# A list schedule in the source for the second mixture and the rest of the last layer 2

## The chip, the cores and the metric

The kernel runs on one core of a Trainium2 chip. The metric is the device time of one execution in microseconds (us). Five engines work side by side, each through its own instruction list in order: PE (TensorE, matmuls), DVE (VectorE), ACT (ScalarE), POOL (GpSimd, which here mostly issues indirect transfers) and SP (which issues the plain transfers). An instruction waits on semaphores that other engines or transfers raise; everything behind it on the same engine waits with it.

## The reference

```python
x = attention(q, k, v)            # B4 H8 S576 D64, causal, window 64, -> (2304, 512)
x = moe(x)                        # 8 experts, weights by Sinkhorn, every expert on every token
# second mixture: each token goes to one expert, at most cap tokens for each
N, D, E, F = (2304, 512, 8, 1024)
cap = N // E                      # 288
logits = x @ w_gate
order = np.argsort(-logits.flatten())
for idx in order:
    tok, e = (int(idx) // E, int(idx) % E)
    if assigned[tok] >= 0 or counts[e] >= cap:
        continue
    assigned[tok] = e
    counts[e] += 1
for e in range(E):
    mask = assigned == e
    h = np.maximum(x[mask] @ w1[e], 0.0)
    out[mask] = h @ w2[e]
```

## The kernel before

Tokens lie in 18 row tiles of 128. Attention and the first mixture take the first 1598 us; they work in blocks of 384 tokens, three products in float16 halves for each product of the reference. The change concerns the rest, called the tail here:

- **The gate of the second mixture.** When the first mixture's last expert has finished a row tile, `gate2` transposes it (L986 on PE, the copy L987 on ACT), multiplies it with the gate's weights (L991) and copies the logits (L992 on DVE); `to_rows` normalises it (L998 on ACT, a chain of small DVE operations L312 to L317, L1005 and L1006 on ACT, L1008 on POOL) and stores it as rows of two float16 halves, `xrows`. For the last six tiles `held_logits` computes the logits ahead from the hidden values (L1052 and L1054 on PE, L1056 to L1059 on DVE), so that routing can begin while 126 matmuls of the last layer 2 (L943) still stand on PE.
- **`route(ph)`** assigns 288 tokens to one expert, the one that fills first, in each of eight phases. Masked logits (L1114 to L1136), then six rounds of a search for a threshold: a comparison `G` of 128x720 on DVE (L1146, L1148), 18 small matmuls on PE that count (L1152), two small DVE operations (L1154, L1155), small matmuls that broadcast the new bound (L1159). Then counts (L1171), the expert's number `widx` (L1185), a prefix sum (L1217), slots (L1221 to L1231), one-hot rows (`oh` L1233, `rh` L1237), 18 matmuls that turn them into row numbers (L1241), `idx` (L1253), three gathers of 96 rows each on POOL (L1258), 24 transposes on PE in three groups of 8 (L1277), and three copies into `xgt`, one on DVE (L1279) and two on ACT (L1281).
- **`ffn(ph)`** has 96 matmuls of layer 1 (L1302) and 96 of layer 2 (L1314), each of 128x288. **`put(ph)`** transposes the result back in three groups (L1324), scales it on ACT (L1326) and stores it with an indirect transfer on POOL (L1328).
- **The weights of an expert** come by four indirect gathers of 1 MB on POOL (L1193) into one of two sets of buffers: the two of layer 1 as soon as `widx` is known, the two of layer 2 behind the three row gathers.

What sets the order: up to the line `man.close()` the source's own list schedule (tasks, each with requests for an engine, a cost and the events on which it waits) emits the instructions. Behind it the framework's scheduler orders what the source emits, and `man.close()` stands ahead of `held_logits` and `second`, so that the tail is in the scheduler's order. It is there that L943 stands between the held logits, and that the rounds of route `ph+1` stand between the matmuls of `ffn(ph)`.

## Time and profile before

| | before |
|---|---|
| median of 3 runs | 1947.3 us (1940.54 to 1947.51) |
| profiled execution, its own time | 1943.79 us |
| its span, first to last instruction | 1942.0 us |
| mean granted clock of TensorE | 0.988 |
| PE busy | 1859.8 us, 96% |
| DVE busy | 1261.4 us, 65% |
| ACT busy | 916.1 us, 47% |
| POOL busy | 110.8 us, 6% |

The shares are means over the whole span; the tail from 1598 us on is 18% of it and has limits of its own. A busy PE includes the time in which the last matmul ahead of a wait runs out of the pipeline. The profiled execution lies 3.5 us under the median of the runs.

### The profile page before, as it was taken

How to read it: one execution, taken by the hardware profiler on the slowest of the kernel's cores; microseconds unless marked ns; L12 is line 12 of the kernel's file. 1: busy time of each engine (PE TensorE's matmuls, PEld its weight loads, DVE VectorE, ACT ScalarE, POOL GpSimd, SP SyncE). 2: the span in 40 equal slices, each digit the busy share in tenths (PEclk: the TensorE clock that was granted, in tenths of full speed). 3: DMA queues.
4: the chain of work that ended last, by engine and by line, in shares of the span. 5: the costliest groups of instructions: out<-in, count | busy, mean ns of one | idle time of the engine just before them, and what ended most of it. 6: DMA issues, size and time to landing. Idle time of an engine off the chain costs nothing.

```text
span 1942.0 us, 39658 instructions
## 1 busy us (share of the span) xinstructions
PE 1859.8 (96%) x15605; PEld 1339.3 (69%) x15605; DVE 1261.4 (65%) x3845; ACT 916.1 (47%) x2493; POOL 110.8 (6%) x142
## 2 busy tenths in 40 slices
PE   6899999999999999999999999999999997899987
PEld 5777755776686766767766867677686773676765
DVE  7877796464666676676667666766747777465540
ACT  6777634552455555554554555455534442222222
POOL 0000000000000000000000000000000113223231
PEclk9999999999999999999999999999999998899999
DMA  8465301140134323323442434234231101435451
GB/s 188 89 131 120 83 1 44 59 160 1 55 120 143 119 93 118 138 88 116 145 136 83 131 117 145 93 99 157 88 104 28 43 20 64 175 123 172 159 211 29
DMA packets 172795, 203.32 MB, mean 105 GB/s; under 512 B 83000, under 2 KB 130104, under 8 KB 168512
## 3 DMA queue, kind: packets, MB, share of 16 engines
q1 hardware_dynamic: 164928, 157.78, 27.4%
q0 software_dynamic: 7680, 43.02, 6.3%
q8 instruction: 122, 2.00, 0.4%
q14 instruction: 65, 0.53, 0.1%
HBM read 143.05 MB, written 57.71 MB: 103 GB/s over the span
## 4 chain that ended last, share of the span: by engine, by line
PE 71%; DVE 11%; issue 6%; DMA 5%; ACT 4%; POOL 2%; SPq 0%; POOLq 0%; ACTq 0%; DVEq 0%
PE p L943 28%; PE p L865 17%; PE pb L865 12%; PE p L1302 4%; PE p L773 3%; DMA w2scr<-st2k 2%; DVE st2k L347 1%; DMA raw<-xrows,idx 1%; PE pb L1152 1%; DVE xl L645 1%; PE p L1314 1%; DMA raw<-in_moe_w_dram 1%; DMA ws<-st2k 1%; PE pb L632 1%; DVE pn L605 1%
## 5 line engine op out<-in xcount | busy, mean ns | idle before, releaser
L943 PE MATMUL p<-w2b,hh 128*128 128x512 f16 x2304 | 686.0, 379 | 0.0
L943 PE MATMUL p<-w2b,hl 128*128 128x512 f16 x1152 | 436.6, 379 | 0.0
L943 PEld LDWEIGHTS <-hh 128*128 128x128 f16 x2304 | 222.1, 99 | 218.2 <-issue 0.2
L865 PEld LDWEIGHTS <-w1b 128*128 128x128 f16 x4032 | 340.3, 98 | 22.2 <-issue 4.0
L865 PEld LDWEIGHTS <-w1x 128*128 128x128 f16 x3024 | 256.3, 98 | 21.1 <-issue 7.4
L865 PE MATMUL p<-th,w1x 128*128 128x192 f16 x1344 | 221.2, 246 | 4.3 <-ACT sa L877 2.2
L865 PE MATMUL pb<-xh,w1b 128*128 128x192 f16 x1344 | 221.3, 246 | 0.0
L943 PEld LDWEIGHTS <-hl 128*128 128x128 f16 x1152 | 112.6, 98 | 135.5 <-issue 0.6
L865 PE MATMUL pb<-xl,w1b 128*128 128x192 f16 x672 | 165.3, 246 | 0.0
L865 PE MATMUL p<-tl,w1x 128*128 128x192 f16 x672 | 165.3, 246 | 0.0
L347 DVE SCALAR_TENSOR_TENSOR st2k<-raw,wsc,st2k 128x512 f16<-128x512 f32 x128 | 91.9, 748 | 51.8 <-ACT st2k L345 51.5
L345 ACT ACTIVATE st2k<-raw,wsc 128x512 f16<-128x512 f32 x128 | 86.5, 713 | 71.3 <-DMA ws<-st2k 58.8
L959 DVE SCALAR_TENSOR_TENSOR acc<-p,SE,acc 128x512 f32<-128x512 f32 x126 | 94.0, 746 | 38.2 <-PE p L943 37.8
L1008 POOL TENSOR_TENSOR st2k<-tmp,st2k 128x512 f16<-128x512 f32 x18 | 24.7, 1370 | 1592.2 <-ACT tmp L1006 1571.1
L746 ACT ACTIVATE hh<-sb 128x192 f16<-128x192 f32 x168 | 61.0, 363 | 111.8 <-DVE sb L909 111.8
L865 PE MATMUL p<-th,w1b 128*128 128x192 f16 x672 | 110.6, 246 | 2.9 <-ACT sc L898 2.9
L746 ACT ACTIVATE hh<-sa 128x192 f16<-128x192 f32 x168 | 60.9, 363 | 107.2 <-DVE sa L883 107.2
L865 PE MATMUL pb<-xh,w1x 128*128 128x192 f16 x672 | 110.6, 246 | 0.0
L865 PE MATMUL p<-xh,w1b 128*128 128x192 f16 x672 | 110.6, 246 | 0.0
L883 DVE TENSOR_TENSOR sa<-pb,sa 128x192 f32<-128x192 f32 x168 | 60.0, 357 | 75.1 <-PE pb L865 72.6
L747 DVE SCALAR_TENSOR_TENSOR hl<-sa,hh 128x192 f16<-128x192 f32 x168 | 60.3, 359 | 72.1 <-ACT hh L746 72.1
L747 DVE SCALAR_TENSOR_TENSOR hl<-sb,hh 128x192 f16<-128x192 f32 x168 | 60.3, 359 | 71.7 <-ACT hh L746 71.7
(309 smaller groups left out, 3381.3 us busy)
## 6 DMA issues: line engine op xcount, KB each, us to landing
raw<-in_moe_w_dram SPq DMA_DIRECT2D x128, 512.0 KB, 5.6
ws<-st2k SPq DMA_DIRECT2D x128, 256.0 KB, 4.5
w2b<-w2scr SPq DMA_DIRECT2D x28, 512.0 KB, 7.1
w2scr<-st2k SPq DMA_DIRECT2D x48, 256.0 KB, 4.5
xrows<-st2k SPq DMA_DIRECT2D x18, 257.0 KB, 3.3
vs<-in_v_dram SPq DMA_DIRECT2D x35, 128.0 KB, 4.1
ldq<-in_q_dram SPq DMA_DIRECT2D x16, 256.0 KB, 4.6
ldk<-in_k_dram SPq DMA_DIRECT2D x16, 256.0 KB, 4.8
```

What stands on the lines that cost most here:

```text
L345: A.activation(hi, src, AF.Copy, scale=sc)
L347: V.scalar_tensor_tensor(lo, src, sc, hi, op0=OP.mult, op1=OP.subtract)
L605: V.tensor_tensor_reduce(pn[:, b, hp], pss[:, hp], mk, 1.0, -3.0e38, OP.add, OP.max, mx[:, u:u + 1])
L746: A.activation(hh[:, f, cols], src, AF.Relu)
L747: V.scalar_tensor_tensor(hl[:, f, cols], src, 0.0, hh[:, f, cols], op0=OP.max, op1=OP.subtract)
L773: PE.matmul(p[:, 0:w], w1v[wi][:, c, fs], x[:, c, ts], start=(n == 0), stop=(n == 3 * DC - 1))
L865: PE.matmul(bank[:, 0:HB], aq[wi][:, c, fs], xq[xi][:, c], start=(start and n == 0), stop=(n == 5), skip_group_check=True)
L883: V.tensor_tensor(t, b3[:, 0:HB], t, OP.add)
L943: PE.matmul(p, h[:, f, js], w2v[wi][:, f], start=(n == 0), stop=(n == 3 * FC - 1))
L959: V.scalar_tensor_tensor(acc[:, i], p, SE[:, e, i:i + 1], acc[:, i], op0=OP.mult, op1=OP.add)
L1008: G.tensor_tensor(xr[:, DM:2 * DM], xs, xr[:, 0:DM], OP.subtract)
L1302: PE.matmul(p[:, 0:CAP], wv1[f // 4][w][:, c, fs], xt[:, x * DC + c], start=(n == 0), stop=(n == 3 * DC - 1))
```

## The change

`man.close()` moves behind `second()`, so that the tail is emitted by the source's own list schedule, in the order of the source, with a cost for each step. For this `route` is cut into `route_a` (up to the slots), `weights_of` (all four gathers of an expert's weights, asked for as soon as `widx` is known) and `route_b` (one-hot rows to `xgt`); `ffn` asks for PE in units of three matmuls, `put` in three steps; the rest of the last layer 2 is a task of its own (`rest`). `to_rows` loses the second ACT copy and the POOL subtraction; one DVE operation of 128x512 does both. Some small operations of `route` move: `ob`, `cap` and `un` are updated ahead of the one-hot rows, `wi`, `wv` and `wp` ahead of the slots, `sv` behind the copies to `xgt`. The spacer's memset on POOL stands ahead of every store.

```diff
     def to_rows(i, x=1, dep=None):
...
+        a = yield Rq("ACT", 0.8, [dep])
         xs = rc["tmp"][:, x]
...
         A.activation(xr[:, 0:DM], acc[:, i], AF.Copy, scale=s)
-        A.activation(xs, acc[:, i], AF.Copy, scale=s)
-        yield 1
-        G.tensor_tensor(xr[:, DM:2 * DM], xs, xr[:, 0:DM], OP.subtract)
+        d = yield Rq("DVE", 0.75, [a.end], wait=0)
+        V.scalar_tensor_tensor(xr[:, DM:2 * DM], acc[:, i], s, xr[:, 0:DM], op0=OP.mult, op1=OP.subtract)
         SP.dma_start(xrows[i * 128:(i + 1) * 128, :], xr)
...
-        gather(*((0, x) for x in range(1 if ph == 0 else 2)))
         V.tensor_scalar(eo, eo, e8, None, op0=OP.is_equal)
-        yield 1
+        ft.add(weights_of(ph, widx, d.end), 2)
...
+    def weights_of(ph, widx, dep):
+
+        ws = wset2[ph % 2]
+        for m, a in ((0, 0), (0, 1), (1, 0), (1, 1)):
+            d = yield Rq("POOL", 1.2, [dep, ("free", ph - 2, m, a) if ph > 1 else "rest" if ph and m else None])
+            G.indirect_dma_start(out=ws[m][:, a * 4096:(a + 1) * 4096], out_offset=None, in_=wscr[m][a],
+                                 in_offset=bass.IndirectOffsetOnAxis(ap=widx[:, :1], axis=0))
...
         for j in range(NJ):
             x = xgb[(ph * NJ + j) % len(xgb)]
-            xd = G.indirect_dma_start(out=x, out_offset=None, in_=xrows[:, :],
-                                      in_offset=bass.IndirectOffsetOnAxis(ap=idx[:, j:j + 1], axis=0))
+            h = yield Rq("POOL", 1.2, [d.end] + [("xr", i) for i in HELD] + [("xgt", ph - 2)] * (ph > 1))
+            G.indirect_dma_start(out=x, out_offset=None, in_=xrows[:, :],
+                                 in_offset=bass.IndirectOffsetOnAxis(ap=idx[:, j:j + 1], axis=0))
...
-        rc["lastx"] = xd.ins
-        gather(*([(0, 1)] if ph == 0 else []), (1, 0), (1, 1))
...
+        ft.add(put(ph), 4)
...
+        ft.add(all_a(), RA)
+        ft.add(all_ffn(), 10)
+        ft.run(lambda: not ft.tasks)
...
     consts_route()
-    man.close()
     for b in range(NB - 2, NB):
         held_logits(b)
     bg.until("finish")
...
     second()
+    man.close()
     late.close()
```

How the instructions stand now is shown at three places.

**The start of the tail, on DVE.** `hs`, `hu` and `lg` take the held logits out of PSUM; `sw` and `tri` are constants of the routing, and `tri` is made from `jpr`, which POOL writes. Before:

```order
L1058 SCALAR_TENSOR_TENSOR hu<-pb,hs,lgh 128x8 x2
L1059 SCALAR_TENSOR_TENSOR lg_91<-pb,hs,hu 128x8
L747 SCALAR_TENSOR_TENSOR hl_82<-sb,hh_81 128x192
L1077 MEMSET sw 40x128 x3
L1059 SCALAR_TENSOR_TENSOR lg_91<-pb,hs,hu 128x8
L1056 TENSOR_SCALAR hs<-SE,gi 128x1 x2
L1058 SCALAR_TENSOR_TENSOR hu<-pb,hs,lgh 128x8 x2
L1059 SCALAR_TENSOR_TENSOR lg_91<-pb,hs,hu 128x8 x2
L1090 TENSOR_SCALAR tri<-jpr 128x128
```

After the change:

```order
L749 SCALAR_TENSOR_TENSOR hl_82<-sb,hh_81 128x192
L1082 MEMSET sw 40x128 x3
L1095 TENSOR_SCALAR tri<-jpr 128x128
L1097 MEMSET ones_19778 128x128
...
L1103 MEMSET AA 128x288
L1103 MEMSET zero 128x18
L1061 TENSOR_SCALAR hs<-SE,gi 128x1
L1063 SCALAR_TENSOR_TENSOR hu<-pb,hs,lgh 128x8
L1064 SCALAR_TENSOR_TENSOR lg_91<-pb,hs,hu 128x8
```

All six groups of `hs`, `hu` and `lg` now stand behind the constants; before, four of the six stood ahead of `tri`. Behind the six groups come three tiles of `gate2` and `to_rows` one after the other, where before one was left at this place, and then the first operation of routing (`lm`). This is the last of the three and the beginning of `lm`:

```order
L994 COPY lg_91<-pb 128x8
L314 TENSOR_SCALAR pbn<-x2m 128x1
L315 TENSOR_SCALAR pbn<-pbn 128x1
L317 TENSOR_SCALAR pcn<-pbn 128x1
L318 TENSOR_SCALAR x2s<-pcn 128x1
L319 TENSOR_SCALAR x2inv<-pcn 128x1
L1007 MEMSET st2k 128x2
L1008 COPY st2k<-x2inv 128x1
L1012 SCALAR_TENSOR_TENSOR st2k<-acc,x2s,st2k 128x512
L1126 TENSOR_TENSOR lm<-lg_91,ob 128x144
```

On PE the six tiles of held logits follow each other without an L943 (now L945) between them, then three times the transposes and the gate's matmuls of `gate2` (now L988, L993), then 30 matmuls of L945, and then the first 18 matmuls of a round.

**The end of a phase, on PE.** The rows are those of one of the middle phases; `pb<-rh,oh` are the 18 matmuls for the row numbers, `pb<-id,raw` a group of eight transposes of gathered rows, `pb<-A,G` a round's matmuls, `ident,yT` a group of `put`; of every run of equal rows the first stands here. Before, 48 matmuls of layer 2 lie between the row numbers' matmuls and the first transposes, three between the groups, and 15 behind the last; the round of the next phase follows:

```order
L1241 MATMUL pb<-rh,oh 96x6
...
L1314 MATMUL p_21612<-hh_81,w2b 128x288
...
L1277 MATMUL pb<-id_19879,raw 128x96
...
L1152 MATMUL pb<-A_21698,G 40x8
...
L1159 MATMUL pb<-fl,sw 128x1
```

After the change 24 matmuls of layer 2 follow the row numbers' matmuls, and the transposes stand in the next phase's first two rounds and `put`:

```order
L1171 MATMUL pb<-A_21612,G 40x8
...
L1413 MATMUL p_21682<-ident,yT 96x128 x4
L1180 LDWEIGHTS sw
L1180 MATMUL pb<-fl,sw 128x1
L1413 MATMUL p_21697<-ident,yT 96x128 x4
L1326 LDWEIGHTS raw
L1326 MATMUL pb<-id_19780,raw 128x96
...
L1413 MATMUL p_21746<-ident,yT 96x128 x4
...
L1383 MATMUL p_21790<-xgt_20013,xh 128x288
```

Behind the first two rounds' matmuls come the transposes of the first and the second group of rows, behind the last group of `put` those of the third, then the third round and layer 1. On DVE the copy of the second group (now L1330) stands between the second and the third `G`.

**The gathers of a phase, on POOL.** `xh`, `xl` (set 0) and `w1b`, `w2b` (set 1) are the weights' buffers, `raw` the gathered rows, `out_dram` the stores. Before:

```order
L1193 DMA w1b<-ws_121,widx 128x4096
L1258 DMA raw<-xrows,idx 96x1028 x3
L1193 DMA w2b<-ws_122,widx 128x4096
L1193 DMA w2b<-ws_123,widx 128x4096
L1328 DMA out_dram<-tmp,idx 2304x512 x3
L1193 DMA xh<-ws_120,widx 128x4096
```

After the change:

```order
L1284 DMA w1b<-ws_120,widx 128x4096
L1284 DMA w1b<-ws_121,widx 128x4096
L1284 DMA w2b<-ws_122,widx 128x4096
L1284 DMA w2b<-ws_123,widx 128x4096
L1316 DMA raw<-xrows,idx 96x1028 x3
L1421 MEMSET spacer 1x1
L1422 DMA out_dram<-tmp,idx 2304x512
```

The two gathers for layer 2 have moved from behind the row gathers to ahead of them, into one burst of four.

## Rows read from the trace of the kernel before

**Rows 1.** Windows: length, busy time of PE, PEld, DVE, ACT, POOL; clock, DMA share, GB/s.

```profile
1640.00:1650.00 10.00, 3.95 (x79) 3.18 (x79) 5.82 (x20) 1.33 (x2) 3.32 (x3) 0.54 0.09 30
1650.00:1660.00 10.00, 5.14 (x68) 3.93 (x68) 3.20 (x10) 1.62 (x2) 4.24 (x5) 0.50 0.82 294
...
1735.00:1770.00 35.00, 33.38 (x371) 24.85 (x370) 21.02 (x83) 8.57 (x17) 9.88 (x10) 1.00 0.45 155
```

**Rows 2.** PE's timeline at the head: start, length, operation, idle time before it.

```profile
1598.29 0.34 PE L1052 MATMUL pb<-w2h,hh 128*128 128x16 f16 x8
...
1609.67 0.61 PE L1152 MATMUL pb<-A,G 128*40 128x8 f16 x18 [0.38 <-DVE st2k L1004]
...
1626.48 0.22 PE L1171 MATMUL pb<-AG,ones 128*128 128x144 f16 x1
...
1637.81 0.97 PE L1241 MATMUL pb<-rh,oh 128*96 128x6 f16 x18 [1.23 <-DVE rh L1237]
...
1658.99 1.14 PE L1302 MATMUL p<-xgt,xh 128*128 128x288 f16 x4
```

**Rows 3.** The last `gate2` and its `to_rows`: timelines of ACT, PE and DVE.

```profile
1593.39 0.60 ACT L987 ACTIVATE tmp<-pb 128x512 f32<-128x512 f32 x1 [0.75 <-PE pb L986]
...
1595.13 0.95 PE L991 MATMUL pb<-wg2s,tmp 128*128 128x8 f32 x8
...
1596.12 0.17 DVE L992 COPY lg<-pb 128x8 f32<-128x8 f32 x1 [2.68 <-PE pb L991]
...
1596.95 0.72 ACT L1005 ACTIVATE st2k<-acc,x2s 128x512 f16<-128x512 f32 x1 [2.35 <-DVE x2s L316]
1597.58 0.70 ACT L1006 ACTIVATE tmp<-acc,x2s 128x512 f32<-128x512 f32 x1
```

**Rows 4.** DVE's timeline at the head, and POOL's first operation there.

```profile
1603.43 0.23 DVE L1090 TENSOR_SCALAR tri<-jpr 128x128 f16<-128x128 f32 x1 [1.93 <-POOL jpr L1089]
...
1605.06 0.74 DVE L959 SCALAR_TENSOR_TENSOR acc<-p,SE,acc 128x512 f32<-128x512 f32 x1
1605.72 0.30 DVE L1114 TENSOR_TENSOR lm<-lg,ob 128x144 f32<-128x144 f32 x1
...
1601.06 1.15 POOL L1008 TENSOR_TENSOR st2k<-tmp,st2k 128x512 f16<-128x512 f32 x1 [7.09 <-issue]
```

**Rows 5.** PE's timeline of one middle phase: its two heads and its waits.

```profile
1692.35 0.61 PE L1152 MATMUL pb<-A,G 128*40 128x8 f16 x18
...
1712.57 0.29 PE L1314 MATMUL p<-hh,w2b 128*128 128x288 f16 x1
1713.08 0.16 PE L1217 MATMUL pb<-tot,tri 128*128 128x2 f16 x1 [0.23 <-DVE tot L1214]
...
1717.63 0.97 PE L1241 MATMUL pb<-rh,oh 128*96 128x6 f16 x18 [0.30 <-DVE rh L1237]
...
1722.79 0.51 PE L1277 MATMUL pb<-id,raw 96*128 96x96 f16 x8 [0.49 <-DMA raw<-xrows,idx]
...
1723.92 0.52 PE L1277 MATMUL pb<-id,raw 96*128 96x96 f16 x8 [0.26 <-DMA raw<-xrows,idx]
...
1725.22 0.51 PE L1277 MATMUL pb<-id,raw 96*128 96x96 f16 x8 [0.42 <-DMA raw<-xrows,idx]
...
1727.51 0.61 PE L1152 MATMUL pb<-A,G 128*40 128x8 f16 x18
```

**Rows 6.** That phase's late copies to `xgt` (DVE, ACT), and POOL's gathers for layer 2.

```profile
1726.63 0.56 DVE L1279 COPY xgt<-pb 128x768 f16<-128x768 f16 x1 [2.57 <-PE p L1314]
...
1726.75 0.81 ACT L1281 ACTIVATE xgt<-pb 128x768 f16<-128x768 f16 x1 [2.60 <-PE p L1314]
...
1723.25 0.96 POOL L1193 DMA_INDIRECT xl<-ws,widx  x1 [0.31 <-issue]
```

**Rows 7.** PE's two long waits of the last phases, from its timeline.

```profile
1870.76 1.63 PE L1302 MATMUL p<-xgt,xh 128*128 128x288 f16 x12 [2.36 <-ACT xgt L1281]
1886.16 0.50 PE L1277 MATMUL pb<-id,raw 96*128 96x96 f16 x8 [3.27 <-ACT xgt L1281]
```

More of the change, by code (lines that the diff above doesn't have):

```diff
@@ L961, in layer2 @@
                 finals.append(i)
-            if i == NT - 1 and not out:
+            if i == NT - 1 and not out and "out" not in rc:
                 bg.done.add(("l2x", e))
@@ L998, in to_rows @@
         A.activation(xs, acc[:, i], AF.Square, accum_out=m)
+        d = yield Rq("DVE", 1.0, [a.end], wait=1.5)
         s = small.tile([128, 1], F32, name="x2s")
@@ L1277, in route, with ws_of, evac_h, evac_y @@
                 PE.transpose(pt[:, c], xg[j][:, c * 128:(c + 1) * 128], rc["id16"][0:R, 0:R])
+            fr = ("l1", ph - 2) if ph > 1 else None
             if j % 2:
+                d = yield dv(0.82, p.end, fr)
                 V.tensor_copy(xt[:, :, j * R:(j + 1) * R], pt)
             else:
+                d = yield Rq("ACT", 0.81, [p.end, fr])
                 A.activation(xt[:, :, j * R:(j + 1) * R], pt, AF.Copy)
-            yield 1
-        PH[ph] = (xt, ws, idx, sv)
+            ft.release("psx", p.idx, d.end)
+        ft.at["xgt", ph] = d.end
+        yield dv(0.5)
+        for j in range(NJ):
+            V.tensor_tensor(sv[:, j:j + 1], xg[j][:, 2 * DM:2 * DM + 2].bitcast(F32), wp[0:R], OP.mult)
+        PH[ph] = (xt, ws_of(ph), idx, sv)
+        ft.at["rows", ph] = d.end
+    def ws_of(ph):
+        return wset2[ph % 2]
     xgb, xgt, otb, yTb, wset2 = [], [], [], [], []
     stores = []
-    def ffn(ph, before):
+    def evac_h(ph, f, p, e):
+        hh, hl = [t[:, :, 0:CAP] for t in hbuf[ph % 2]]
+        a = yield Rq("ACT", 0.42, [e.end])
+        A.activation(hh[:, f], p[:, 0:CAP], AF.Relu)
+        d = yield dv(0.46, a.end)
+        V.scalar_tensor_tensor(hl[:, f], p[:, 0:CAP], 0.0, hh[:, f], op0=OP.max, op1=OP.subtract)
+        ft.release("ps1", e.idx, d.end)
+        ft.at["hb", ph, f] = d.end
+    def evac_y(ph, d, p, e, idx):
+        a = yield Rq("ACT", 0.42, [e.end, ("put", ph - 1) if ph else None])
+        A.activation(yTb[0][:, d], p[:, 0:CAP], AF.Copy)
+        ft.release("ps2", idx, a.end)
+        ft.at["y", ph, d] = a.end
+    def ffn(ph):
+        while ("rows", ph) not in ft.at:
+            yield IDLE
         xt, ws, idx, sv = PH[ph]
@@ L1324, in put @@
                 PE.transpose(p[0:R, d * 128:(d + 1) * 128], yT[:, d, j * R:(j + 1) * R], ident)
+            if j == NJ - 1:
+                ft.at["put", ph] = e.end
+            a = yield Rq("ACT", 0.68, [e.end], "ot")
             ot = otb[(ph * NJ + j) % len(otb)]
             A.activation(ot, p[0:R], AF.Copy, scale=sv[:, j:j + 1])
+            ft.release("ps2", e.idx, a.end)
+            g = yield Rq("POOL", 1.3, [a.end])
             G.memset(rc["spacer"], 0.0)
@@ L1332, in put, with evac_rest, rest @@
             stores.append(st)
-            yield
+    def evac_rest(i, p, t, idx):
+        d = yield dv(0.75, t)
+        V.scalar_tensor_tensor(acc[:, i], p, SE[:, E - 1, i:i + 1], acc[:, i], op0=OP.mult, op1=OP.add)
+        ft.release("ps2", idx, d.end)
+        x = len(finals) % 2
+        e = yield from to_rows(i, i % 2, d.end)
+        ft.at["xr", i] = e + 3.6
+    def rest():
+        k = 12 - pend[0][1]
+        tick = rc["tick"]
+        for g, n in ((pend[0][0], k), (layer2(E - 1, NB - 1), 12)):
+            for x in range(12 - n, 12):
+                e = yield Rq("PE", 1.31, [], "ps2" if x % 4 == 0 else None)
+                if x % 4 == 0:
+                    tick[0] = e.idx
+                rc["pe"] = e
+                next(g)
+        for _ in g:
+            pass
     def second():
@@ L1351, in second, with all_a, all_ffn @@
             rc[n] = late.enter_context(tc.tile_pool(name=n, bufs=x, space=PSUM))
-        first = route(0)
-        for x in first:
-            if x == "rows":
-                break
-        rest()
-        def route_all():
-            for ph in range(E):
-                for _ in first if ph == 0 else route(ph):
-                    yield 1
-                bg.done.add(("r", ph))
-                yield 1
-        bg.start("route", route_all())
-        before = iter(())
-        for ph in range(E):
-            bg.until(("r", min(ph + 1, E - 1)))
-            ffn(ph, before)
-            before = put(ph)
-        for _ in before:
-            pass
+        assert not bg.tasks, bg.tasks
+        bg.hold = True
+        rc["tick"] = [0]
+        ft.rel["ps2"].append(None)
+        rc["out"] = lambda i, p: ft.add(evac_rest(i, p, rc["pe"].end, rc["tick"][0]), 1)
+        def all_a():
+            for ph in range(E):
+                while ("begun", ph - AHEAD) not in ft.at and ph >= AHEAD:
+                    yield IDLE
+                yield from route_a(ph)
+        def all_ffn():
+            yield from rest()
+            ft.at["rest"] = rc["pe"].end
+            for ph in range(E):
+                ft.at["begun", ph] = ft.t
+                yield from ffn(ph)
+        ft.at["free", -1, 0, 0] = 0.0
+        ft.add(all_a(), RA)
+        ft.add(all_ffn(), 10)
+        ft.run(lambda: not ft.tasks)
+        del rc["out"]
     wgr = abase.tile([128, DC, E], F32, name="wgr")
```

183 lines of the change are left out of this document (114 added, 69 removed).

## The prediction

> **What bounds the kernel now.** I read the windows first, to find where PE is not full, then PE's timeline in those stretches, and then the engine that each of its waits names. Up to 1598 us nothing of weight changes: PE is full there, and the edits move work on ACT, POOL and DVE beside it. The tail has three parts. In the head PE stands half idle: of the twenty microseconds from 1640 to 1660 it is busy for 9.1, at a granted clock of 0.54 and 0.50, the lower level (1.2 GHz of 2.4) [rows 1]. The routing of phase 0 is a chain there: first round at 1609.67, counts at 1626.48, row numbers at 1637.81, layer 1 at 1658.99 [rows 2]. Then come five middle phases that repeat each other, 35.2 us from head to head (1692.35 to 1727.51) [rows 5], with PE busy for 33.4 of 35 [rows 1]: PE is the bound, and its small waits are what can be had. Last come the phases from 1868 us on, in which PE waits 2.36 and 3.27 us for ACT's copies to `xgt` [rows 7].
>
> The profiled execution took 1943.79 us for a span of 1942.0, and the median of the runs, 1947.3, is 1.0018 times that. I work out a change of the span and scale at the end.
>
> **The middle phases.** The price of a matmul of 128x288 is (1.63 - 0.29)/11 = 0.122 us [rows 7, 5]. PE's five waits of a phase are listed with 0.23, 0.30, 0.49, 0.26 and 0.42, together 1.70 us [rows 5]. That is not all that they cost: the listed idle begins when the last matmul has run out, 0.29 after its start, where a next one could have begun after 0.122. The first wait shows it: 1712.57 to 1713.08 is 0.51, and less 0.122 that is 0.39, not 0.23. So each wait costs 0.17 more, and all five 1.70 + 0.85 = 2.5 us.
>
> After the change 42 matmuls of layer 2 (5.1 us) stand between the counts and the prefix sum, and 45 (5.5 us) between this and the row numbers, where before these two were 4.55 us apart with both waits in it (1713.08 to 1717.63) [rows 5]. I take both waits as covered. For the gathered rows I count from the row numbers on: these 0.83, 24 matmuls 2.9, a round 0.55, two groups of `put` 1.1 and a bound 0.1 put PE at the first transposes at 5.5. Before, the rows were there at 5.16, 6.29 and 7.59 (1722.79, 1723.92 and 1725.22 less 1717.63) [rows 5]. PE comes to the second group at about 6.4 and to the third at about 7.6. So these three waits are covered too, without the 48 + 3 + 3 matmuls that covered part of them before.
>
> There is a new wait. On DVE the copy of the second group stands ahead of the third `G`, and behind this `G` PE's third round. Transposes done at 6.9, copy 0.56 [rows 6], `G` about 0.97: 8.5, where PE arrives at 7.95. That costs 0.6. Behind it layer 1 needs ACT's copy of the third group, 7.6 + 0.5 + 0.81 = 8.9, and PE is there at 9.1. So a phase gains 2.5 - 0.6 = 1.9 us, and five of them **9.5 us**.
>
> This holds only if the copies start when their transposes end. Before they did not. The second group's transposes ended at 1723.92 + 0.52 = 1724.44 [rows 5] and DVE's copy started at 1726.63; ACT's copy of the third started 1.0 us after its transposes (1725.73 to 1726.75) [rows 6]. The two wait on nothing in the program but their transposes. Both started within 3.4 to 3.5 us of 1723.25, when POOL issued the first of the two gathers of weights that stand behind the row gathers [rows 6]. The late phases show the same at the same place. So I put the lag down to those gathers, and they no longer stand there. Before, the lag was hidden by the 15 matmuls behind the last transposes (1.8 us); that cover is gone, so if the lag stays, it shows.
>
> The Trainium skill, page "SBUF — State Buffer", section "SBUF: two separate sides", speaks against this reading: it has DVE and GpSimd share one pair of ports as an exclusive lock, but says that "PE, ACT, and DVE's dedicated pair never wait on anyone". ACT's copy was 1.0 us late all the same, so by that rule the gathers are not what holds ACT, and the lag could stay where it is; that is the first rival below.
>
> **The four gathers in one burst.** The two for layer 2 now run ahead of the rows, some 2.1 MB more. At 294 GB/s for a share of 0.82 [rows 1], full engines move 358 GB/s, so four gathers take 11.7 us, and begin to flow about 1.5 us after `widx`, thus end 13.2 behind it. The row gathers are issued about 10.3 us behind `widx` (an estimate: 87 matmuls of 0.122 from the counts to the row numbers, 1.9 from there to the issue, less some 2.2 from the counts to `widx`), and land 3.2 us later, at 13.5. So I take no delay. Bounds: 0, and 5.9 us if the rows had to wait for both added gathers in full.
>
> **The head.** Three of the `gate2` that stood in the stream of layer 1 now stand behind the held logits. Each is 0.95 for its matmuls [rows 3] and about 0.3 for its transposes, so PE reaches the held logits 3.75 us earlier, at 1594.5 instead of 1598.29 [rows 2]. There it must wait. The held logits leave PSUM through DVE, four banks hold them, and on DVE the constants stand ahead, with `tri`, which waited 1.93 us for POOL's `jpr`; POOL's first operation came at 1601.06, behind 7.09 us of its own [rows 4]. Moved 3.75 earlier, `tri` is through at about 1599.9, and the six tiles at about 1602. Then the three `gate2` come one after the other, and each `to_rows` ahead of the next on ACT: copy to matmuls about 0.65, matmuls to logits 0.99 (1595.13 to 1596.12), DVE's chain 0.83 (to 1596.95), ACT's copy 0.63, together 3.1 [rows 3]. Three of them end at 1611. PE has 3.75 us of work in those 9, so its clock probably falls, as it did at 0.54 in the idle stretch later [rows 1]. Thirty matmuls of 128x512 (0.217 each by their columns) are 6.5 us, with some 3 us for the lower level 9.5: first round at 1620.5, against 1609.67.
>
> From there 96 such matmuls, 20.8, and six rounds, 3.3: counts at 1645, 18 us later than before. From the counts to the row numbers it was 11.3 us [rows 2], a chain on DVE with little else behind it: 1656. From there a middle phase's 7.6 to the last transposes [rows 5], their 0.5, ACT's copy 0.8: layer 1 at 1665, 6 us late. Before, phase 0 took 33.4 from there to the next head (1658.99 to 1692.35) [rows 2, 5]; now 192 matmuls are 23.4, five rounds 2.8, row numbers and small ones 1.3, and some 3.5 for the lower clock at its start, 31. The head thus costs **+4 us**. Bounds: -1 if the clock stays up ahead of the rounds and DVE's chain runs in 9; +10 if PE stays at the lower level through all of the rest.
>
> **The end.** The two waits of rows 7 are both for ACT's copies, late behind bursts of row gathers, weights and stores on POOL. With the weights of the last two experts ahead of their rows I take 4 of these 5.6 us: **-4 us**, bounds 0 and -5.6.
>
> **Costed at nothing.** `to_rows` saves ACT 0.70 [rows 3] and POOL 1.15 [rows 4] for each of 18 tiles and costs DVE 0.75 (as the accumulation of that shape, 0.74 [rows 4]). Fourteen or so lie beside full PE stretches. Uncovered it would be 0.75 in each of the head's chains, of which only the last is on the path; that is inside the head's bounds. The memsets of the spacer, the moved updates of `ob`, `cap`, `un` and `wp`, and `sv` behind the copies are DVE and POOL operations of 0.15 to 0.2 in stretches with slack; all on the path they would be 1 us a phase.
>
> **Sum:** +4 - 9.5 - 4 = -9.5 us; 1943.8 - 9.5 = 1934.3, times 1.0018 that is 1938.
>
> **Rivals.**
> - *The lag of the copies stays.* The third `G` is then ready at 6.9 + 2.2 + 0.56 + 0.97 = 10.6, PE waits 2.7 instead of 0.6, and a phase gains nothing. For it: ACT's lag, which shared ports don't explain. Against it: the first copy of the phase, ahead of those gathers, had no lag. +4 - 4 + 1 = +1: 1946.
> - *The head costs nothing.* If POOL's 7 us pass earlier, since no subtraction stands ahead of `jpr`, PE stays busy and the clock up. Then -13.5: 1934, or less.
> - *The burst delays the rows.* If the row gathers wait behind the added 2.1 MB, each phase loses the delay. It decides from 1.9 us on, where the middle phases' gain is gone; at 4 us, between the bounds, five phases lose 20 and the sum is +10.5: 1958. Against it: in the estimate above the rows land just behind the burst.
> - *The change does not do what it says.* Routing is allowed to run three phases ahead, but in the order it is one phase ahead, as before; so nothing is to be had from that, and nothing is in the sum.
>
> **Chances.** The forecast 0.45, the lag stays 0.25, the head free 0.15, the burst 0.15. Half a per cent, 9.7 us, is about what a measurement of this kernel can tell from no change. The forecast lies almost on that bound, so half of its chance counts as faster, nearly all the rest as the same; with the third case faster is 0.40. The same is the rest of the forecast and the first rival, 0.43; slower is the burst and a little of the head's upper bound, 0.17. The range reaches from 1927 (the head free and its waits covered) to 1953 (the lag, with the head's upper bound). The likeliest case by itself is 1932 to 1944.
>
> **What would show it.** Right: heads about 33.2 us apart; copies of the second group that start within 0.2 us of their transposes; no idle of PE ahead of the row numbers' matmuls; third rounds that wait about half a microsecond. In the head: PE all but idle for some 9 us ahead of the rest of layer 2, first round near 1620, layer 1 of phase 0 near 1665. Wrong: a pitch of 35 with waits ahead of the third round (the lag), of 37 with waits for `raw` (the burst), or a head that reaches phase 1 before 1692.

## The result, and the profile after

| | before | after |
|---|---|---|
| median, measured together | 1945.45 us (4 runs) | 1972.34 us (4 runs, 1969.13 to 1977.62) |
| ratio to before | | 1.0145, 95% interval [1.0113, 1.0176] |
| profiled span | 1942.0 us | 1975.8 us |
| mean granted clock | 0.988 | 0.969 |

The change makes the kernel slower by 1.45%; the forecast was half a per cent faster. The kernel before itself had medians between 1933.84 and 1946.54 us in six sets of runs, also between two sets under one chip number (1946.54 and 1935.47). So below each kernel is compared by the ratio with the runs of before that were taken together with it.

The heads of phases 1 to 6 (here the first operation of the next phase's `put`; in four of them a round stands half a microsecond ahead of it) stand at 1702.04, 1741.14, 1778.89, 1818.36, 1857.25 and 1896.23 us. Before, the first of them was 1692.35 and the pitch 35.1 [rows 5]. So the 33.8 us of the span come from three places: the head of the tail 1702.04 - 1692.35 = **+9.7** (forecast +4), the five middle phases (1896.23 - 1702.04)/5 = 38.8 instead of 35.1, **+18.7** (forecast -9.5), and the end **+5.4** (forecast -4). The two medians differ by 26.9 us, 7 less than the two profiled spans; the execution of after that was profiled is the slowest of its four. For the experiments the pitch is counted from layer 1 to layer 1, as the mean of four middle phases; so counted it is 38.7 for the changed kernel.

PE's timeline at the head of the tail, after:

```profile
1600.24 0.39 PE L1057 MATMUL pb<-w2h,hh 128*128 128x16 f16 x8 [5.31 <-DVE lg L1064]
...
1611.52 1.88 PE L993 MATMUL pb<-wg2s,tmp 128*128 128x8 f32 x8 [1.18 <-ACT tmp L989]
...
1648.38 0.22 PE L1199 MATMUL pb<-AG,ones 128*128 128x144 f16 x1 [1.18 <-DVE AG L1194]
...
1658.86 1.36 PE L1304 MATMUL pb<-rh,oh 128*96 128x6 f16 x15 [4.80 <-DVE rh L1299]
1663.56 0.59 PE L1171 MATMUL pb<-A,G 128*40 128x8 f16 x13 [3.11 <-DVE G L1164]
1667.50 0.74 PE L1326 MATMUL pb<-id,raw 96*128 96x96 f16 x7 [1.61 <-DMA raw<-xrows,idx]
1671.31 1.12 PE L1383 MATMUL p<-xgt,xh 128*128 128x288 f16 x4 [0.76 <-ACT xgt L1333]
```

PE waits 5.31 us for the held logits, whose DVE operations now stand behind `tri`. The gate's eight matmuls take 1.88 us where they took 0.95 [rows 3], half the speed. The first round came at 1621.22.

One middle phase in PE's timeline, which answers to [rows 5]:

```profile
1736.78 0.93 PE L1304 MATMUL pb<-rh,oh 128*96 128x6 f16 x18
...
1740.61 0.61 PE L1171 MATMUL pb<-A,G 128*40 128x8 f16 x18
1741.14 0.64 PE L1413 MATMUL p<-ident,yT 128*96 128x128 f32 x4
1743.35 0.16 PE L1180 MATMUL pb<-fl,sw 40*128 40x1 f16 x1 [1.56 <-DVE fl L1175]
1743.44 0.64 PE L1413 MATMUL p<-ident,yT 128*96 128x128 f32 x4
1744.83 0.51 PE L1326 MATMUL pb<-id,raw 96*128 96x96 f16 x8 [0.74 <-DMA raw<-xrows,idx]
...
1748.70 0.76 PE L1171 MATMUL pb<-A,G 128*40 128x8 f16 x18 [0.32 <-DVE sv L1338]
1749.39 0.90 PE L1383 MATMUL p<-xgt,xh 128*128 128x288 f16 x3
```

The two waits ahead of the row numbers are gone, as forecast. But from 1740.61 to 1749.39, 8.8 us, PE has only transposes, three rounds and two bounds (the small matmuls that broadcast a round's new bound); no layer 2 is left. In that stretch are all the waits. The windows there (columns as in [rows 1]), and then windows of whole phases, two of the four and the sum of all four:

```profile
1742.00:1744.00 2.00, 0.65 (x5) 0.39 (x4) 0.77 (x3) 0.68 (x1) 0.59 (x3) 1.00 0.81 218
1744.00:1746.00 2.00, 1.25 (x30) 1.08 (x30) 0.52 (x1) 1.31 (x2) 1.78 (x3) 0.96 0.16 47
1746.00:1748.00 2.00, 2.00 (x20) 1.60 (x19) 1.20 (x4) 0.19 (x1) 0.67 (x2) 0.50 0.59 174
...
1750.00:1752.00 2.00, 2.00 (x12) 1.04 (x10) 0.70 (x3) 0.00 (x0) 0.92 (x1) 0.50 0.25 66
```
```profile
1702.00:1741.00 39.00, 36.71 (x388) 27.94 (x387) 25.25 (x85) 8.68 (x18) 11.66 (x15) 0.87 0.42 152
1741.00:1780.00 39.00, 35.91 (x383) 27.23 (x380) 24.02 (x83) 8.60 (x18) 11.51 (x15) 0.91 0.42 149
...
sum 155.00, PE 144.11 PEld 108.91 DVE 97.20 ACT 34.00 POOL 43.19; mean PE 36.03 PEld 27.23 DVE 24.30 ACT 8.50 POOL 10.80
```

PE is busy 0.65 of two microseconds, then the granted clock drops to 0.50, the lower level, and stays there for some six, into layer 1. Four phases (1702 to 1857) have PE busy for 144.1 of 155: 36.0 and 2.7 idle for each, against 33.4 and 1.6 before [rows 1]. So of 3.7 us a phase, **2.7 are busy time, for the same matmuls with the clock at its lower level for some six, and 1.1 are idle**.

DVE in the same phase, from the one-hot rows to the first two rounds:

```profile
1735.89 0.27 DVE L1299 TENSOR_TENSOR rh<-ohj,tp 128x108 f16<-128x108 f32 x1
1736.08 0.30 DVE L1126 TENSOR_TENSOR lm<-lg,ob 128x144 f32<-128x144 f32 x1
...
1738.97 0.17 DVE L1151 SCALAR_TENSOR_TENSOR hm<-sx,un 128x18 f32<-128x18 int32 x1
1739.18 0.35 DVE L1152 TENSOR_SCALAR hm<-hm 128x18 f32<-128x18 f32 x1
1739.56 0.91 DVE L1164 TENSOR_TENSOR G<-hm,cj 128x720 f16<-128x720 f32 x1
1742.94 0.16 DVE L1174 TENSOR_TENSOR f<-pb,cap 40x8 f32<-40x8 f32 x1 [2.48 <-PE p L1413]
```

All of the next phase's masked logits stand between `rh` and the first `G`, which starts 3.67 us behind `rh` and ends as the 24 last matmuls of layer 2 run out (1740.47 and 1740.39). And `f`, which needs the round's matmuls alone, starts 1.7 us after these ended (1740.61 + 0.61). The row names a transpose of `put` (L1413), the last that PE ended before; even from its end, 1741.78, `f` is 1.2 us late.

At the end, PE's two longest waits, and one of ACT:

```profile
1899.52 0.74 PE L1326 MATMUL pb<-id,raw 96*128 96x96 f16 x7 [2.31 <-DMA raw<-xrows,idx]
...
1915.10 1.14 PE L1383 MATMUL p<-xgt,xh 128*128 128x288 f16 x8 [3.01 <-DVE hl L1353]
```
```profile
1913.58 0.68 ACT L1418 ACTIVATE tmp<-p,sv 96x512 f32<-96x512 f32 x1 [4.59 <-DMA out_dram<-tmp,idx]
```

The wait of 3.01 for `hl` comes from ACT. ACT waits 4.59 us for a store of `put`'s result, issued at 1905.13 behind the last expert's four gathers of weights and its rows, and takes out layer 1's values only then.

### The profile page after: what moved, and what is told of

It reads as the page before. It is cut to its first block, busy times and chain, and to the rows that moved or that the text cites. A ratio compares the mean times of both kernels' runs of the same rounds, so it can differ in the third digit from the quotient of the medians.

```text
span 1975.8 us, 39600 instructions
## 1 busy us (share of the span) xinstructions
PE 1879.7 (95%) x15605; PEld 1356.3 (69%) x15605; DVE 1289.9 (65%) x3862; ACT 904.7 (46%) x2475; POOL 87.4 (4%) x124
## 4 chain that ended last, share of the span: by engine, by line
PE 76%; DVE 11%; DMA 4%; issue 4%; ACT 3%; POOL 1%; SPq 0%; POOLq 0%; ACTq 0%; DVEq 0%
PE p L945 31%; PE p L867 17%; PE pb L867 12%; PE p L1383 4%; PE p L775 3%; DMA raw<-xrows,idx 2%; DMA w2scr<-st2k 2%; PE pb L1171 1%; PE pb L634 1%; DVE st2k L349 1%; PE p L1399 1%; PE pb L993 1%; DVE xl L647 1%; PE pb L623 1%; DVE oh L1294 1%
## 5 line engine op out<-in xcount | busy, mean ns | idle before, releaser
L945 PE MATMUL p<-w2b,hh 128*128 128x512 f16 x2304 | 686.3, 379 | 0.0
L945 PE MATMUL p<-w2b,hl 128*128 128x512 f16 x1152 | 437.1, 379 | 0.0
L945 PEld LDWEIGHTS <-hh 128*128 128x128 f16 x2304 | 222.0, 99 | 218.8 <-issue 1.1
L945 PEld LDWEIGHTS <-hl 128*128 128x128 f16 x1152 | 112.7, 98 | 136.4 <-issue 0.8
L961 DVE SCALAR_TENSOR_TENSOR acc<-p,SE,acc 128x512 f32<-128x512 f32 x120 | 89.6, 747 | 38.9 <-PE p L945 38.6
L775 PE MATMUL p<-xh,w1b 128*128 128x384 f16 (+1 forms) x512 | 101.9, 289 | 4.4 <-DVE hl L757 3.8
```

Source lines behind the costliest of these rows:

```text
L775: PE.matmul(p[:, 0:w], w1v[wi][:, c, fs], x[:, c, ts], start=(n == 0), stop=(n == 3 * DC - 1))
L945: PE.matmul(p, h[:, f, js], w2v[wi][:, f], start=(n == 0), stop=(n == 3 * FC - 1))
L961: V.scalar_tensor_tensor(acc[:, i], p, SE[:, e, i:i + 1], acc[:, i], op0=OP.mult, op1=OP.add)
```

## The experiments

**The order of the gathers.** e1 and e2 start from the changed kernel and move the two gathers for layer 2 behind the row gathers, or behind the copies to `xgt`:

```diff
-        for m, a in ((0, 0), (0, 1), (1, 0), (1, 1)):
+        for a in range(2):
...
+        ft.add(weights_of(ph, WI[ph], h.end, 1), 2)
```

This is e1. `weights_of` now does one layer, `m`, and is asked for twice, the second time (the last line) behind the row gathers. In e2 that line stands behind the copies, with `d.end` in place of `h.end`.

> After the change, with one edit: the two gathers of layer 2's weights are issued behind the three row gathers, as before the change, and not ahead of them. Theory 'burst' (four gathers in a row delay the rows from 3.2 to about 6 us and hold up PE's signals to DVE in the first round; the idle that follows lets the clock fall): rows land 3.2 to 3.7 us after their issue, no wait of PE for raw rows above 0.3 us, the first bound comes without 1.5 us of idle, the hold-up moves to the copies; pitch from 38.9 to about 36, the whole 12 to 18 us faster than the changed kernel, about 1957. Theory 'layout' (the phase's head is a chain of small rounds, put and transposes without large matmuls between, and idles whatever the gathers do): pitch 38.4 to 39.4, within 4 us of 1972.

> After the change, with one edit: the two gathers of layer 2's weights are issued only behind the copies to xgt, when layer 1 begins. Theory 'burst': rows land within 3.7 us, no hold-up of the first round nor of the copies, the clock stays up at the phase's head; pitch 33.5 to 35, the whole 20 to 27 us faster than the changed kernel, about 1949; a new wait is possible where layer 2 begins, if the weights land late. Theory 'layout': pitch 38.4 to 39.4, about 1972.

Measured: e1 1978.78 us, ratio 1.0170 [1.0152, 1.0187]; e2 1981.44, 1.0179 [1.0162, 1.0197]; both pitches 39.1. In e1 the waits for `raw` are gone, the waits ahead of the bound (1.4) are not, and there are new ones ahead of the second bound (0.7 to 1.55). The burst is not what costs the 18.7 us. e4 puts the same burst into the kernel before:

```diff
-        gather(*((0, x) for x in range(1 if ph == 0 else 2)))
+        gather((0, 0), (0, 1), (1, 0), (1, 1))
...
-        gather(*([(0, 1)] if ph == 0 else []), (1, 0), (1, 1))
```

> The kernel before, with one part of the change alone: all four gathers of weights behind widx, ahead of the row gathers. Theory 'bare head' (the burst's delay of the rows hurts little by itself; what costs is that a phase's head has no large matmuls to cover its waits, and that the clock falls there): the rows land up to 3 us later, PE waits for raw 1 to 3 us in layer 2 where it now waits 1.2, the clock stays at 1.0; pitch from 35.1 to 36 to 38 at most, the whole 0 to 12 us slower, about 1952. Rival 'burst': pitch near 39, 18 us slower, about 1964.

Measured: 1948.44, 1.0014 [0.9997, 1.0031]: on the whole no cost that can be told from nothing. The pitch of the middle phases is 36.3 instead of 35.1, so there the burst costs about 1.1 a phase; the tail is in the scheduler's order here, which also came out anew.

**The gathers' traffic.** e5 is the changed kernel and leaves out the gathers of the weights of phases 2 to 7.

> After the change, with the weights' gathers of phases 2 to 7 left out (these phases compute with the weights of phases 0 and 1). It shows the phase's head without their traffic. Theory 'burst': rows land in 3.2 us, DVE's first f of a phase follows its matmuls within 0.2 us, clock 1.0 throughout, pitch 33 to 34.5, span about 1947 to 1952. Theory 'layout': pitch above 37 and the clock still falls at the head.

Measured once: 1960.68 us beside 1946.54 of before; pitch 37.3. The gathers have about 1.4 us a phase; the wait ahead of the bound (1.8) and the fall of the clock to 0.50 stay.

**The head.** e3 puts the held logits ahead of the constants and takes the spacing out of `to_rows` (one of its pauses is shown; the others go likewise, and one of 1 us comes in ahead of its last operation):

```diff
-    consts_route()
     for b in range(NB - 2, NB):
         held_logits(b)
+    consts_route()
...
-        d = yield Rq("DVE", 1.0, [a.end], wait=1.5)
+        d = yield Rq("DVE", 1.0, [a.end], wait=0)
```

> After the change, with the head's two edits: the held logits are emitted ahead of the routing's constants, and to_rows asks for no pauses between its steps, so that the three gates stand in layer 1's stream again. Theory 'head by sum' (idle and the lower clock ahead of the rest of layer 2 cost about 14 us there): held logits end about 1600, first round at 1605 to 1610 instead of 1621, layer 1 of phase 0 at about 1659 instead of 1671; the whole 10 to 14 us faster, about 1960; the pitch of 38.9 stays. Rival: the chain from the counts to the rows takes the time back, and the whole gains under 4 us.

Measured: 1964.59, 1.0091 [1.0062, 1.0121]. First round 1612.04 (9.2 earlier), layer 1 of phase 0 at 1661.56 (9.8 earlier). The first `put` stands at 1692.98, where before has its first head at 1692.35. The ratio falls by 0.0054, 10.5 us, which is the head's loss within the intervals. Which of the two edits gives it back, e3 doesn't separate.

**The clock.** e6 puts matmuls without use into the head of each phase, so that PE isn't idle there:

```diff
+            if j < 2 and ph < E - 2:
+                for n in range((12, 6)[j]):
+                    PE.matmul(p[:, 0:CAP], wset2[ph % 2][1][:, 0:128], ...)
```

> After the change, with 18 matmuls of 128x288 on old data added at the head of each phase but the last (12 ahead of put's first group, 6 ahead of its second; their results are overwritten, the output is the same): 2.2 us of PE work where PE idles for 2.3 to 3. It asks what the fall of the clock costs by itself. Theory 'bare head': the clock stays at or near 1.0 through the head (now 0.5 to 0.7 for six microseconds), pitch 38.9 to about 35.5 to 36.5, the whole 12 to 17 us faster than the changed kernel, about 1957. Rival 'waits only' (the idle, not the clock, is the loss): pitch stays at 38.5 to 39.5 or grows, 1972 to 1976.

Measured: 1979.94, 1.0177 [1.0152, 1.0203]. The fill held the clock in one phase of four; windows of two phases:

```profile
1741.00:1780.00 39.00, 37.53 (x421) 29.27 (x420) 26.46 (x95) 8.73 (x18) 11.50 (x15) 1.00 0.45 161
1780.00:1819.00 39.00, 37.60 (x393) 28.22 (x390) 24.06 (x84) 8.42 (x17) 10.38 (x14) 0.91 0.42 153
```

The phase at 1.00 took 36.4 us (layer 1 at 1752.94 and 1789.32), 2.3 less than after's mean, although its 18 matmuls take 2.2 themselves (0.122 each); the mean of the four is 37.75. So the clock's share is real. The whole is not faster, because other phases grew (phase 1 from 40.1 to 42.5 us, phase 6 from 37.0 to 43.1), for a cause that I did not find; so the whole doesn't price the clock.

**The first rounds.** e7 computes the masked logits and keys of phase ph+1 in the gaps of phase ph's prefix sum and slots, so that less stands between `rh` and `G`. `masked` has ten steps, and each `nx()` emits one. The edit also moves the update of `un` and changes prices in the list, so PE's order comes out anew too:

```diff
+        nxt = masked(ph + 1) if not last else iter(())
...
         V.tensor_tensor(AA[:, 0], AA[:, 0], AG[:, 1], OP.add)
+        nx()
         if not last:
             V.tensor_tensor(AA[:, 1], AG[:, 0], AG[:, 1], OP.subtract)
+        nx()
```

> After the change, with ten small DVE operations of the next phase's routing (masked logits and the split of the key) moved from behind the one-hot rows to between the dependent operations of the prefix sum and the slots, so that DVE's chain from the counts to the next phase's first G is about 3.5 us shorter; the list schedule then puts the first two rounds among the last matmuls of layer 2. Theory 'bare head': PE's waits at the head under 1 us in all, the clock at 1.0, pitch 34 to 35.5, the whole 17 to 24 us faster than the changed kernel, about 1951. Rival 'hold-up' (signals from PE held up by POOL's gathers cost the same wherever the rounds stand): pitch 37.5 or more, at most 7 us faster.

> e3_head and e7_masked_early together. If head and middle phases are separate terms, the gains add: 8 us from the head and those of e7, about 1941 to 1945, no slower than the kernel before. If the head's gain is taken back by the phases, about 1950.

Measured: e7 1953.11, 1.0034 [1.0022, 1.0046], by the ratios about 22 us less than the changed kernel, pitch 33.7. e8 is e3 and e7 together: 1939.83, 0.9972 [0.9959, 0.9985]. Windows of e7, two phases:

```profile
1711.00:1745.00 34.00, 32.88 (x373) 25.27 (x373) 22.38 (x84) 8.39 (x18) 10.60 (x14) 1.00 0.46 163
1745.00:1778.00 33.00, 32.30 (x369) 24.81 (x368) 21.36 (x84) 8.08 (x17) 9.67 (x14) 1.00 0.45 160
```

The clock stays at 1.00 and the idle is 0.9 a phase. e13 is the same kernel as e8, run again beside other runs of before, and shows both kinds of phase in one execution:

> e8_both unchanged, on the chip of this call. If the later weights of e9 did the harm there, the ratio is 0.997 again, within 0.002. Rival, that the chip did it: near 1.004.

Measured: 1939.93, 1.0019 [1.0009, 1.0029]; so e8 equals before within 0.3%, and the sign differs between the two sets. The kernel took the same time in both (1939.83 and 1939.93); what differs is before (1945.91 and 1935.47). PE's timeline in e13 at the same place of a phase, and a late wait; then windows:

```profile
1719.08 0.93 PE L1340 MATMUL pb<-rh,oh 128*96 128x6 f16 x18
...
1720.33 0.61 PE L1194 MATMUL pb<-A,G 128*40 128x8 f16 x18
...
1723.39 0.61 PE L1194 MATMUL pb<-A,G 128*40 128x8 f16 x18
...
1726.20 0.61 PE L1194 MATMUL pb<-A,G 128*40 128x8 f16 x18
...
1729.22 1.26 PE L1419 MATMUL p<-xgt,xh 128*128 128x288 f16 x9 [0.45 <-ACT xgt L1369]
...
1793.42 0.52 PE L1362 MATMUL pb<-id,raw 96*128 96x96 f16 x8 [2.11 <-DMA raw<-xrows,idx]
```
```profile
1729.00:1762.00 33.00, 32.38 (x370) 25.03 (x370) 21.93 (x84) 8.21 (x18) 10.53 (x14) 1.00 0.45 164
1762.00:1798.00 36.00, 33.51 (x367) 25.99 (x367) 21.68 (x81) 8.15 (x18) 10.62 (x13) 0.94 0.44 156
...
1794.00:1796.00 2.00, 2.00 (x30) 1.61 (x29) 0.31 (x2) 1.47 (x2) 0.21 (x1) 0.50 0.00 0
```

The first round starts 1.25 us behind the row numbers instead of 3.83, and layer 2 stands between the rounds; layer 1 is reached in 10.1 us instead of 12.6. Two phases take 33.2 us and two 36.3. These two have a wait for rows at the head, 2.11 and 1.60 us, where the others wait 0.34; so 1.8 us more of waiting cost 3.1, and behind the wait the granted clock is 0.50.

**A known delay.** e14 and e15 put ten dependent operations on `hm` ahead of the first `G` of phases 1 to 6, in the kernel before and in the changed one:

```diff
             V.tensor_scalar(hm, hm, -1.0, None, op0=OP.add)
+            if 0 < ph < E - 1:
+                for x in range(10):
+                    V.tensor_scalar(hm, hm, 0.0, None, op0=OP.add)
```

> The kernel before with ten more dependent small DVE operations (add 0 to the selection keys hm of phases 1 to 6, about 0.2 us each, 2 us in all) ahead of the first G of each of these phases. There G is ready about 8 us before PE uses it, so my theory expects no change, within 3 us of before. Rival, that the time goes with DVE's work as such: 6 x 2 = 12 us longer.

> The changed kernel with the same ten operations at the same place. If the routing loop through DVE is the bound of the middle phases there, each of six phases grows by 2 us: about 12 us longer than the changed kernel, between 8 and 14, pitch 40.8. Rival, that PE's own stream, the rows or the clock bound them: within 3 us of the changed kernel, pitch 38.8.

Measured: e14 1939.89, 1.0023 [1.0011, 1.0035], 4.4 us; e15 1982.83, 1.0237 [1.0217, 1.0257]. DVE and PE in a phase of e15:

```profile
1785.22 2.42 DVE L1155 TENSOR_SCALAR hm<-hm 128x18 f32<-128x18 f32 x10
```
```profile
1788.64 0.61 PE L1174 MATMUL pb<-A,G 128*40 128x8 f16 x18 [2.31 <-DVE G L1167]
```

Of 2.42 added, PE waits 2.31 for the first `G`: no slack. In the middle phases of e14 there is no wait ahead of this round at all. But e14 missed its expectation by 1.4 us (its pitch is 36.0). e15 took 10.5 us more than the changed kernel, a time within the expected 8 to 14 (by the ratios it is 18, since before differs between the two sets). But 4 of these us arise in the head, ahead of the first added operation, and the pitch grew by 1.0 to 39.7, not by 2: the wait of 1.56 ahead of the bound and the one for `raw` were gone. So the routing chain alone is not the bound, as I had it; the bare head is.

**The end, and what can be had.** e9 is e8 with the last expert's weights held back until the copies to `xgt` of the phase before; e10 is e9 with the rest of the last layer 2, in the head, in steps of three matmuls; e11 is e8 with e1's order of gathers.

> e8_both, with the last expert's four gathers of weights held back until the copies to xgt of phase 6 are done. At the end of e8_both PE waits 2.2 us for a group of put and 4.0 for raw, while POOL issues rows and weights in one run and DVE and ACT start what they wait for late. Theory 'hold-up' (gathers close to the handshakes cost): both waits go to under 1.5 us in all, the whole 4 to 5 us faster than e8_both, about 1935. Rival: the late weights of phase 7 are waited for later, no gain.

> e9_w7late, with the rest of layer 2 emitted in units of three matmuls, not six, so that a round of routing in the head needs 9 to 12 of its matmuls for cover and not 18, and 27 are left for the stretch between the counts and the prefix sum. Theory 'the head is bound by PE's units in the rounds and by DVE's chain behind the counts': rounds 3.3 to 3.6 us apart instead of 4.8, counts at 1631 instead of 1639, layer 1 of phase 0 at about 1656, the whole 5 to 7 us faster than e9_w7late, about 1929. Rival: the rows of the last tiles, stored behind the rest, are then what layer 1 waits for; gain under 2 us.

> e8_both, with the gathers of layer 2's weights behind the row gathers again, as before the change. Theory 'bare head' (the order of the gathers costs little once large matmuls cover the rounds): pitch within 0.5 us of e8_both's 33.7, the whole within 3 us of it, 1937 to 1943. Rival 'burst': 5 to 15 us faster, about 1930.

Measured in one set: e9 1943.79, 1.0047 [1.0031, 1.0063]; e10 1939.66, 1.0028 [1.0015, 1.0040]; e11 1962.96, 1.0151 [1.0127, 1.0175]. In e9 and e10 the wait moves to the last expert's rows (5.67 and 6.90 us); e9 has no gain over the same kernel without it (e13, 1.0019). e11 is far off its expectation. Its PE waits inside layer 1, for values that ACT and DVE take out late, and ACT in turn waits for a store of `put`'s result:

```profile
1741.15 1.40 PE L1424 MATMUL p<-xgt,xh 128*128 128x288 f16 x6 [2.81 <-DVE hl L1394]
```
```profile
1739.63 0.68 ACT L1459 ACTIVATE tmp<-p,sv 96x512 f32<-96x512 f32 x1 [5.84 <-DMA out_dram<-tmp,idx]
```

In each of e11's five middle phases ACT's third scaling of `put` waits 5.8 to 7.3 us for such a store, in e13 1.1 to 1.6: with layer 2's weights behind the rows, the stores stand behind these gathers. So the burst ahead of the rows, which I had put down as a risk, is the better order once the head is mended. e12 is e8 with the steps of three alone, e17 the same again, e16 adds that the last expert's weights come behind its rows. The steps of three are those of e10, in the head; the middle phases' `ffn` had units of three already, so what is expected of e12 below speaks of another edit than it has. This is what e16 adds:

```diff
+        if ph == E - 1 and ph not in WI:
+            WI[ph] = widx
+            return
...
+        if ph == E - 1:
+            ft.add(weights_of(ph, WI[ph], h.end), 2)
```

> e8_both with layer 2 of the middle phases emitted in steps of three matmuls instead of six (half the step, half its price in the list), and without the later weights of e9. Fine steps matter (a small matmul on PE stands at most 0.4 us behind where it could, instead of 0.75): pitch 33.0 instead of 33.7, ratio 0.992 to 0.995 of before. Rival, that e10's low profile came from the weights that it moved: the pitch stays at 33.7 and the ratio at 0.997, as e13.

> e12_both_fine with all four gathers of the last expert's weights behind that expert's own row gathers. In e12 the first of them was issued at 1849.76, ahead of the rows of the expert before, and PE then waited 6.11 us for these rows. If the weights' traffic holds the rows, that wait goes to 1 us or less and no wait as long comes later, since layer 1 of the last expert starts 27 us after its rows: 4 to 6 us shorter than e12, ratio 0.996 to 0.998 of before where e12 has 0.9995. Rival: the wait only moves to the last expert's rows, as in e9 and e10 (5.67 and 6.90 there): no gain.

> e12_both_fine unchanged, beside e16 on the same chip: 0.9995 of before, within 0.002.

Measured: e12 1934.85, 0.9995 [0.9982, 1.0008], pitch mostly 33.4; e17 1934.76, 0.9992 [0.9980, 1.0005]; e16 beside it **1928.42, 0.9960 [0.9945, 0.9975]**. In e12 layer 1 of phase 0 comes 1.5 us earlier than in e13 (1657.91 for 1659.40); why its middle phases lack e13's two of 36.3, these runs don't show. PE's longest wait of the late phases, in e17 and then in e16:

```profile
1860.97 1.46 PE L1362 MATMUL pb<-id,raw 96*128 96x96 f16 x16 [4.04 <-DMA raw<-xrows,idx]
```
```profile
1857.59 0.51 PE L1369 MATMUL pb<-id,raw 96*128 96x96 f16 x8 [1.99 <-DMA raw<-xrows,idx]
```

e16 is faster than before and than the changed kernel, and takes 6.3 us less than e17. The wait for rows fell to 2, not to 1 as expected; the gain comes at the end (layer 1 of phase 5 at 1827.49 in e16 and 1828.82 in e17, of phase 7 at 1868.65 and 1876.07).

## Why the prediction was wrong

**The middle phases: the step that failed** is the count from the row numbers to layer 1, "a round 0.55, two groups of `put` 1.1 and a bound 0.1 put PE at the first transposes at 5.5". The 24 matmuls and the round came nearly as counted (3.83 us behind the row numbers, against 3.73). The bound did not: it is no 0.1 of PE but waits for DVE's `f` and `fl`, and came at 1743.35, 2.7 us behind its round's start; 1.56 of that PE waited, and this wait is the late start of `f`. The rows landed 6.2 us after their gather's issue (1738.61 to 1744.83) instead of the 3.2 that I took from before, behind 2 MB more: 0.74. The third `G`, where I had put 0.6, cost 0.32. Above all, I took every matmul at full clock: I saw the lower level in the head, where PE idled, and did not ask what nearly nine microseconds of transposes and waits in each phase would do. So layer 1 was reached 12.6 us behind the row numbers, and a phase took 38.8 us where I had 33.2: PE's busy time grew by 2.7 us, its idle time by 1.1.

I had also read the waits of before as what can be had and not asked what covers them. Before, 69 matmuls of layer 2 stood behind the row numbers (48, twice 3, 15); with 24, whatever is late next is bare. That is shown by e7: with the same gathers, the same burst and the same `ffn`, with the masked logits out of the way, the rounds stand among layer 2 again, the clock stays up and the pitch is 33.7, near the 33.2 forecast. (The list's prices moved with it, so what e7 shows is the covered head as a whole, not the ten operations alone.) e15 shows from the other side that the first round had no slack, e14 that before it had enough to take 2.4 us without a wait.

**The late starts** behind POOL's gathers were seen before the change ("the lag"), with the gathers of layer 2 as the cause. That cause fell: in the changed kernel they are ahead of the rows, and now `f` is 1.7 us late and ACT's first scaling of `put` 1.25 (1743.03, its matmuls done at 1741.78); e5 without any such gather in these phases has them as well (a wait of 1.8 ahead of the bound). ACT's row and POOL's first and last row gather of that phase of the changed kernel:

```profile
1743.03 0.68 ACT L1418 ACTIVATE tmp<-p,sv 96x512 f32<-96x512 f32 x1 [1.91 <-PE p L1413]
```
```profile
1738.61 0.93 POOL L1316 DMA_INDIRECT raw<-xrows,idx  x1 [5.30 <-DVE sx L1144]
...
1741.58 0.92 POOL L1316 DMA_INDIRECT raw<-xrows,idx  x1 [0.30 <-issue]
```

The first rival was thus right that the lag stays, but at another place, and for a price that no rival had. The sentence of the Trainium skill that I quoted against my reading, page "SBUF — State Buffer", section "SBUF: two separate sides", speaks of ports; ACT starts late here as well as DVE, so what is late is not explained by the port that DVE shares with GpSimd. No run here tests the page's rule itself. What holds those late starts up stays open. But the order of the instructions alone does not make them, as e8 and e13, one kernel in two sets, show. A round and its `f` at the same place of a phase, in e8 and then in e13, with the row gathers at the same place too:

```profile
1760.44 0.61 PE L1194 MATMUL pb<-A,G 128*40 128x8 f16 x18 [0.29 <-issue]
```
```profile
1761.76 0.16 DVE L1197 TENSOR_TENSOR f<-pb,cap 40x8 f32<-40x8 f32 x1 [1.37 <-PE pb L1194]
```
```profile
1756.57 0.61 PE L1194 MATMUL pb<-A,G 128*40 128x8 f16 x18
```
```profile
1757.21 0.16 DVE L1197 TENSOR_TENSOR f<-pb,cap 40x8 f32<-40x8 f32 x1 [1.14 <-PE pb L1194]
```

`f` starts 0.71 us behind the round's end in e8 and 0.03 in e13. In the sets in which before took 1945 to 1947 us, all kernels but e4 have an `f` that is more than 0.6 us late, up to 4.5, and always near POOL's gathers or stores; in the sets in which before took 1934 to 1936 (e9 to e17) none is more than 0.05 late, with gathers in issue too. So something outside the kernel has part in it. In e8 the late start costs nothing that shows (pitch 33.7), because layer 2 covers it. In e15, which has no late starts, the pitch is 39.7 and the clock falls all the same, behind a wait of 2.31 for `G`; so a bare head does not need them to be dear. The changed kernel itself ran in no set without them, so how much of its 38.8 they make is not shown.

**The head: right in kind, under-sized**: +9.7 for +4. First round 1621.2 (forecast 1620.5), counts 1648.4 (1645), row numbers 1658.9 (1656), layer 1 1671.3 (1665), 30.7 us from there to the phase's end (31). The missing terms are two. The rounds took 27.2 us instead of 24.5, at full clock (1.00 from 1620 to 1648): bounds, breaks between layer 2 and the rounds, and the wait of 1.18 ahead of the counts. From the row numbers to layer 1 it took 12.45 instead of 9, with the wait of 3.11 for `G` in it: the same masked logits as in the middle phases. e3 gives the head's loss back, within the noise, by order alone.

**The end: wrong in sign**, +5.4 for -4. I took the two waits of [rows 7] as gone because the weights come earlier; early weights of the last expert stand ahead of its rows and of the stores of `put`, and PE waits 2.31 for the rows and, through ACT, 3.01 for a store. e16 shows on the base of e12 that late weights give back 6.3 us; in the changed kernel itself this was not tried, so there the cause is argued.

**Right**: the two waits ahead of the row numbers were covered; the third round's wait; the burst alone costs nothing measurable on the whole (e4); PE reached the held logits at 1593.2 for 1594.5, and `tri` was through at 1598.8 for 1599.9. One sum of the first rival has a slip: +1 gives 1948, not 1946.

## What to carry to other kernels

When work that covers a phase's start is moved to cover an earlier wait, list what stands bare afterwards and price it at half the clock, not only by its waits. In an order written out by hand, look what stands on the vector engine between the last step of one iteration and the first of the next: ten small operations that could have run in the gaps of an earlier chain cost about 20 us here (e7). A transfer that is needed later should be issued later, behind the small one that is needed first (e16 against e17). But small stores queue behind it too, and what was harmless in one order can be dear in another: the same move cost 5 us by the ratios in the changed kernel (e1) and 25 in the mended one (e11 against e13).
